# Sixteen weight subtractions on GpSimd instead of VectorE, and another buffer for the last weight tile

## The chip, the core and the metric

The kernel runs on one core of a Trainium2 chip. A core has five engines that run at the same time and meet by semaphores: TensorE (PE; its weight loads are listed as PEld), VectorE (DVE), ScalarE (ACT), GpSimd (POOL) and SyncE (SP), which here issues the DMAs. The metric is the device time of one execution in microseconds (us), as the median of several runs.

## The reference

Three parts follow each other, over 8 batches of 576 tokens, all in float32.

```python
# 1: attention in chunks of 64 tokens, 8 heads of 64
scores = scale * q_c @ k_c.T ; attn = softmax(scores) ; out = attn @ v_c
# 2: gated feed-forward, 512 -> 1024 -> 512, with a convolution of 3 taps along the tokens
h = maximum(x @ w_in, 0)
conv_out = sum_k conv_w[k] * shifted(h, k)
x = (h * sigmoid(conv_out)) @ w_out
# 3: FFT over tokens and features, normalisation, feed-forward 512 -> 2048 -> 512
u = x + real(fft(fft(x, axis=1), axis=2))
un = (u - mean(u)) / sqrt(var(u) + 1e-6)
y = u + maximum(un @ w_ch1, 0) @ w_ch2
```

The weights come as float64 bits, which the kernel turns into float32 itself.

## The kernel before

Matmuls run in a reduced float32 (`F32R`). To keep the precision, a factor is split into a high half and a low half: ScalarE casts the tile to `F32R` (the high half, `h`), VectorE subtracts that from the tile (the low half, `l`); this is `split` (L278). A product is then three matmuls: high times high, high times low, low times high.

The tokens of the first two parts go through in ten blocks (`NBLK`): one of 256 tokens, eight of 512, one of 256. Block 0 uses the plain float32 weights (`m_unit0`, L457, and the branch at L528); from block 1 on the split ones are used. In block 0 everything starts at once:

- `load_weight` (L344) fetches 16 tiles of 128x512, alternately of `w_in` and `w_out`, each as 512 KB of 64-bit words into a tile `wide`, and `to_float32` (L287) makes a float32 tile of it: L292, L293, L295 and L296 on VectorE, L294 on ScalarE. The float32 tiles lie in buffers that later hold other things (`early`, L340: `t`, `u`, `f..`, `fz`, `ds`, `xlo`, `xhi`, `dd`, `fw`), and so do some of the `wide` ones; the others share the ring of two buffers that is named `wide` in pool `w`.
- `attention` (L371) makes the scores (L393), their maxima (L398), the exponentials (L404), sums and division (L407 to L409), a transpose (L418, L421); `values` (L425) multiplies with v (L435) and, from block 1 on, splits the result: the cast at L442 on ScalarE, the subtraction at L444 on VectorE. There are two L444 for each half of a block's heads, so four for block 1.
- `m_step` (L451) multiplies with `w_in` (L459 in block 0, L468 later) for each of eight feature tiles f, goes through ReLU (L493), the middle tap (L498), the other two taps on VectorE (L488), tanh (L505) and the gate (L507), and from block 1 on splits the gated tile into `gh` and `gl` (L279, L280). GpSimd carries three edge columns from one block to the next (L492, L497). In block 0 it also calls `split_weight` (L353), which splits the weight tile that has just been used for the last time in float32.
- `x_step` (L518) multiplies with `w_out` (L531 in block 0, L537 later), and in block 0 splits that weight tile too.
- `load_dft` (L313) brings the transform matrices, with a cast on ScalarE (L323) and a subtraction on VectorE (L324); they land in the tile `fw`, which held the last weight tile in float32.

The order of the work is not that of the code. `Plan` records every operation with its engine, an estimated cost in nanoseconds, a priority and the tiles that it reads and writes. `emit` then plays the program through with these costs and gives each engine its instructions in the order that comes out. On the chip each engine runs its list strictly in order and waits at semaphores. A tile's next user waits for all users of the buffer before it.

Of the kernel before, what the change touches and what calls it, by code (L numbers as in the profile page):

```python
# [8 lines left out]
F32 = mybir.dt.float32  # L9
F32R = mybir.dt.float32r  # L10
I64 = mybir.dt.int64
U32 = mybir.dt.uint32
ACT = mybir.ActivationFunctionType
ALU = mybir.AluOpType
# [86 lines left out]
class Plan:  # L101
# [10 lines left out]
    def buf(self, pool, tag, bufs, shape, dtype=F32):  # L112
        return Buf(self, pool, tag, bufs, shape, dtype)

    def op(self, eng, cost, fn, prio, r=(), w=(), after=(), nbytes=0, spare=0):
        o = Op()
        o.spare = spare
        o.eng, o.cost, o.fn, o.prio, o.nbytes, o.seq = eng, cost, fn, prio, nbytes, len(self.ops)
        o.slots = [b for b in w if b.tag in self.ANY_ORDER and not b.writers]
        deps = {}  # L120
        for b in r:
            assert b.writers and not b.closed, b.tag
            for d in b.writers:
                deps[d] = True
        for b in w:
            assert not b.closed, b.tag
            if not b.writers:
                if b.pool in self.opened:
                    deps[self.opened[b.pool]] = True
                if b.before is not None:  # L130
                    for d in b.before.writers + b.before.readers:
                        deps[d] = True
                if b.previous is not None and b.previous not in w:
                    deps.setdefault(b.previous.writers[0], False)
            for d in b.writers + b.readers:
                deps[d] = True
        for d in after:
            deps[d] = True
        for b in r:
            for x in (b, b.base) if b.base else (b,):  # L140
                x.readers.append(o)
        for b in w:
            for x in (b, b.base) if b.base else (b,):
                x.writers.append(o)
        o.held = [b for b in {id(b): b for b in (*r, *w)}.values() if b.tag in self.ANY_ORDER]
        for b in o.held:
            b.left += 1
        o.deps, o.users = deps, []
        for d in deps:
            d.users.append(o)  # L150
        o.left, o.ready, o.end = len(deps), 0.0, None
        self.ops.append(o)
        return o
# [64 lines left out]
def act_cost(n, psum=False, scalars=0):  # L218
    return (51 if psum else 93) + n / 1.2 + 93 * scalars
# [7 lines left out]
def kernel(  # L227
# [15 lines left out]
    pe, dve, act, pool, sp = nc.tensor, nc.vector, nc.scalar, nc.gpsimd, nc.sync  # L243
    plan = Plan()
    buf, op = plan.buf, plan.op
# [23 lines left out]
    def load(dst, src, nbytes, prio, r=(), after=()):  # L269
        return op("SP", 450, lambda: sp.dma_start(out=dst(), in_=src()), prio, r=r, w=[dst], after=after, nbytes=nbytes)  # L270

    def vop(n, fn, prio, r, w, fast=False, scalars=0):
        return op("DVE", dve_cost(n, fast, scalars), fn, prio, r=r, w=w)

    def aop(n, fn, prio, r, w, psum=False, scalars=0, after=()):
        return op("ACT", act_cost(n, psum, scalars), fn, prio, r=r, w=w, after=after)

    def split(h, l, src, n, prio, psum=False, cut=lambda t: t, after=()):  # L278
        aop(n, lambda: act.copy(out=cut(h()), in_=cut(src())), prio, [src], [h], psum, after=after)  # L279
        vop(n, lambda: dve.tensor_tensor(cut(l()), cut(src()), cut(h()).bitcast(F32), op=ALU.subtract), prio, [src, h], [l])  # L280
# [6 lines left out]
    def to_float32(f, x, wide, n, prio, view=lambda t: t):  # L287

        word = lambda t, k: t.rearrange("p (n two) -> p n two", two=2)[:, :, k]
        lo, hi = lambda: word(wide().bitcast(U32), 0), lambda: word(wide().bitcast(U32), 1)  # L290
        ff, fb, xb = lambda: view(f()), lambda: view(f()).bitcast(U32), lambda: x().bitcast(U32)
        vop(n, lambda: dve.tensor_scalar(xb(), hi(), 3, 0x3FFFFFF8, op0=ALU.logical_shift_left, op1=ALU.bitwise_and), prio, [wide], [x], fast=True)  # L292
        vop(n, lambda: dve.scalar_tensor_tensor(fb(), in0=hi(), scalar=0xC0000000, in1=xb(), op0=ALU.bitwise_and, op1=ALU.bitwise_or), prio, [wide, x], [f])  # L293
        aop(n, lambda: act.activation(out=x(), in_=word(wide().bitcast(F32), 1), func=ACT.Abs), prio, [wide], [x])  # L294
        vop(n, lambda: dve.scalar_tensor_tensor(fb(), in0=lo(), scalar=29, in1=fb(), op0=ALU.logical_shift_right, op1=ALU.bitwise_or), prio, [wide, f], [f])  # L295
        vop(n, lambda: dve.scalar_tensor_tensor(ff(), in0=x(), scalar=LEAST_NORMAL, in1=ff(), op0=ALU.is_ge, op1=ALU.mult), prio, [x, f], [f])  # L296


    def weight(pool_name, tag, bufs):
        return tuple(buf(pool_name, tag + k, bufs, [128, 512], F32R) for k in "hl")  # L300
# [39 lines left out]
    early = [("s", "t", 2), ("s", "t", 2), ("s", "u", 2), ("s", "u", 2)]  # L340
# [3 lines left out]
    def load_weight(src, dst, prio):  # L344
        n = len(wi) + len(wo)
        f = buf(*early[n], [128, 512])
        dst.append([f])
        k = n % 5
        wide = buf(*(early[13 + k] if k < 3 and n < 13 else ("w", "wide", 2)), [128, 512], I64)
        load(wide, lambda: src, 524288, prio - (16.2 if n < 3 else 6))  # L350
        to_float32(f, buf("d", *(("wf", 2) if n % 3 else ("wx", 1)), [128, 512]), wide, 512, prio)

    def split_weight(w, tag, prio, after):  # L353
        f = w[0]
        w[:] = weight("w", tag, 8)
        split(*w, f, 512, prio, after=after)

# [91 lines left out]
    def m_step(i, f, prio):  # L451
# [19 lines left out]
        if i:  # L471
            done = op("PE", mm_cost(n, passes=12), m_unit, prio, r=[*wi[f], *(t.buf for hp in range(0, HP, 2) for t in x0[i, hp])], w=[acc], after=m_last)
            m_last[:] = [done]
        else:
            for hp in range(HP):
                done = op("PE", mm_cost(n, passes=4), lambda hp=hp: m_unit0(hp), prio, r=[wf, x0[i, hp][0].buf], w=[acc], after=() if hp else m_last)
                m_last[:] = m_last if hp else [done]
            split_weight(wi[f], "wi", prio + 6, [done])
# [34 lines left out]
    xacc, xlo, xhi, x_last, pieces = {}, {}, {}, {}, []  # L513
# [4 lines left out]
    def x_step(i, f, prio):  # L518
# [27 lines left out]
        if not i:  # L546
            split_weight(wo[f], "wo", prio + 6, [done])
# [484 lines left out]
    for f in range(FT):  # L1032
        load_weight(w_in[:, f, :], wi, -2 + f)
        load_weight(w_out[:, f, :], wo, 0 + f)
# [66 lines left out]
    for c in range(NCH):  # L1101
        t = start + span * c
        begun = []
        for g in range(FG):
            begun.append(group(c, g, t + 7 * g))
            if (c, g) in LATE:
                n = LATE.index((c, g))
# [125 lines left out]
```

## Time and profile before

| what | value |
|---|---|
| median of 3 runs | 1338.38 us (1335.93 to 1339.33) |
| profiled execution | 1338.54 us, span from first to last instruction 1336.8 us |
| mean granted TensorE clock | 0.995 of full speed |
| busy: PE, DVE, ACT, POOL | 1300.0, 1025.7, 765.7, 109.5 us |
| chain that ended last | PE 89%, DVE 6%, ACT 2% |

Busy time is the time in which an engine had an instruction under way. Consecutive instructions of one engine overlap a little in the records, so a sum of durations can be larger than the time that they took. The chain is followed back from the last instruction to what released each step. An engine's short idle times are listed with what ended them. Spans on GpSimd are rough, and a wait inside one of its instructions is part of its record.

### The profile page before, as it was taken

The page shows a single profiled execution, that of the slowest core. Times are in us where ns is not written, and L with a number is a line of the kernel's source. Part 1 is how long each engine was busy: PE and PEld are TensorE (multiplying, and loading weights), DVE is VectorE, ACT ScalarE, POOL GpSimd, SP SyncE. Part 2 cuts the span into 40 slices and gives each one's busy share as a digit, 9 for nine tenths or more (in the row PEclk, how much of TensorE's full clock was granted, in tenths as well). Part 3 has the DMA queues.
Part 4 walks back from the last instruction along what each step waited for, and adds up shares of the span by engine and source line. Part 5 has one row for each costly group of instructions (what it writes and reads, how often), then busy time and mean ns, then how long its engine had stood idle before and what let it go on. Part 6 is the DMA issues. An engine that isn't in the chain of part 4 may idle for free.

```text
span 1336.8 us, 26161 instructions
## 1 busy us (share of the span) xinstructions
PE 1300.0 (97%) x9888; PEld 1164.6 (87%) x9888; DVE 1025.7 (77%) x1832; ACT 765.7 (57%) x1902; POOL 109.5 (8%) x247
## 2 busy tenths in 40 slices
PE   5899999999999999999999999999999999999998
PEld 3678888788888888888999888888899999999998
DVE  7997979878886777787978768774598887777873
ACT  5968767657685755565766646566644333333331
POOL 1121312201120211120000000000000000000000
PEclk9999999999999999999999999999999999999999
DMA  9435142434423031337765766778655455455441
GB/s 327 148 128 174 42 149 92 159 104 146 148 72 99 17 111 45 100 128 233 220 211 184 227 193 198 209 223 279 195 177 168 137 174 161 139 174 147 154 142 40
DMA packets 155327, 206.29 MB, mean 154 GB/s; under 512 B 10304, under 2 KB 103104, under 8 KB 155200
## 3 DMA queue, kind: packets, MB, share of 16 engines
q1 hardware_dynamic: 155200, 204.61, 48.7%
q8 instruction: 78, 1.28, 0.4%
q14 instruction: 49, 0.40, 0.1%
HBM read 130.51 MB, written 74.06 MB: 153 GB/s over the span
## 4 chain that ended last, share of the span: by engine, by line
PE 89%; DVE 6%; ACT 2%; issue 1%; DMA 0%; SPq 0%; ACTq 0%; DVEq 0%
PE x L933 22%; PE x L1000 16%; PE o L468 14%; PE x L537 13%; PE o L1000 12%; PE o L933 4%; PE o L666 3%; PE o L699 2%; PE o L832 1%; PE o L721 1%; PE o L393 1%; DVE cv L488 1%; PE o L418 1%; PE o L435 1%; ACT th L279 0%
## 5 line engine op out<-in xcount | busy, mean ns | idle before, releaser
L279 ACT CAST sxh<-raw 128x1024 fp32r<-128x1024 f32 (+1 forms) x143 | 146.0, 1028 | 193.6 <-PE o L1000 84.3
L280 DVE TENSOR_TENSOR sxl<-raw,sxh 128x1024 fp32r<-128x1024 f32 (+1 forms) x143 | 169.3, 1193 | 26.7 <-ACT sxh L279 26.7
L933 PE MATMUL x<-sxh,th 128*128 128x512 f32 (+1 forms) x480 | 177.5, 370 | 0.8 <-ACT sum L917 0.6
L468 PE MATMUL o<-x,wih 128*128 128x512 f32 (+1 forms) x576 | 175.8, 388 | 1.8 <-ACT at L421 0.7
L933 PE MATMUL x<-sxh,tl 128*128 128x512 f32 (+1 forms) x480 | 176.6, 368 | 0.0
L933 PE MATMUL x<-sxl,th 128*128 128x512 f32 (+1 forms) x480 | 176.5, 368 | 0.0
L1000 PE MATMUL x<-tl,sxh 128*128 128x256 f32 x576 | 163.2, 283 | 0.0
L1000 PE MATMUL x<-th,sxl 128*128 128x256 f32 x576 | 163.1, 283 | 0.0
L1000 PE MATMUL x<-th,sxh 128*128 128x256 f32 x576 | 163.1, 283 | 0.0
L488 DVE SCALAR_TENSOR_TENSOR cv<-h,cw,cv 128x1 f32<-128x1 f32 (+30 forms) x272 | 129.0, 494 | 25.9 <-ACT cv L498 25.2
L468 PEld LDWEIGHTS o<-x,wih 128*128 128x128 f32 x576 | 104.1, 189 | 24.0 <-ACT h L493 1.5
L1000 PE MATMUL o<-tl,sxh 128*128 128x256 f32 x432 | 122.4, 283 | 0.0
L1000 PE MATMUL o<-th,sxl 128*128 128x256 f32 x432 | 122.4, 283 | 0.0
L1000 PE MATMUL o<-th,sxh 128*128 128x256 f32 x432 | 122.4, 283 | 0.0
L537 PE MATMUL x<-gh,woh 128*128 128x512 f32 (+1 forms) x288 | 112.6, 391 | 0.0
L1000 PEld LDWEIGHTS x<-th,sxh 128*128 128x128 f32 x576 | 110.7, 192 | 0.2
L1000 PEld LDWEIGHTS x<-tl,sxh 128*128 128x128 f32 x576 | 110.7, 192 | 0.0
L1000 PEld LDWEIGHTS x<-th,sxl 128*128 128x128 f32 x576 | 110.7, 192 | 0.0
L537 PE MATMUL x<-gh,wol 128*128 128x512 f32 (+1 forms) x288 | 110.3, 383 | 0.0
L468 PE MATMUL o<-x,wil 128*128 128x512 f32 (+1 forms) x288 | 110.0, 382 | 0.0
L537 PE MATMUL x<-gl,woh 128*128 128x512 f32 (+1 forms) x288 | 109.6, 381 | 0.2
L909 DVE TENSOR_TENSOR u<-x,u 128x256 f32<-128x256 f32 (+2 forms) x112 | 55.8, 498 | 67.4 <-PE x L1000 38.7
(280 smaller groups left out, 2955.4 us busy)
## 6 DMA issues: line engine op xcount, KB each, us to landing
raw<-h_scr SPq DMA_DIRECT2D x72, 512.0 KB, 5.0
h_scr<-sum SPq DMA_DIRECT2D x72, 256.0 KB, 3.0
u<-u_scr SPq DMA_DIRECT2D x66, 256.0 KB, 3.4
qk<-in_qk SPq DMA_DIRECT2D x32, 512.0 KB, 5.1
h_scr<-sum SPq DMA_DIRECT2D x48, 192.0 KB, 2.5
out_y<-u SPq DMA_DIRECT2D x35, 256.0 KB, 2.5
v<-in_v_in SPq DMA_DIRECT2D x32, 256.0 KB, 3.9
wide<-in_w_ch SPq DMA_DIRECT2D x16, 512.0 KB, 4.4
```

What stands on the lines that cost most here:

```text
L279: aop(n, lambda: act.copy(out=cut(h()), in_=cut(src())), prio, [src], [h], psum, after=after)
L280: vop(n, lambda: dve.tensor_tensor(cut(l()), cut(src()), cut(h()).bitcast(F32), op=ALU.subtract), prio, [src, h], [l])
L393: pe.matmul(s[h]()[half[u], 4 * w + 2 * p + j, :], t[half[h], w, 0, ks], t[half[h], w, 1, ks], start=True, stop=True)
L418: pe.transpose(tps()[:, k, :], flat[:, 512 * c + 128 * k:512 * c + 128 * k + 128], ident)
L468: pe.matmul(acc(), w[:, ws], x, start=k == 0, stop=k == 11)
L488: vop(hi - lo, lambda: dve.scalar_tensor_tensor(cv()[:, lo:hi], in0=h()[:, off + k - 1 + lo:off + k - 1 + hi], scalar=tap(k), in1=cv()[:, ...
L537: pe.matmul(accs[d](), w[:, dsl], x, start=f == 0 and k == 0, stop=f == FT - 1 and k == 2)
L666: pe.matmul(acc()[:rows, :], x, w, start=k == 0 and n == 0, stop=k == 1 and n == 2)
L699: pe.matmul(accs[sine]()[:rows, :], w, x, start=n == 0, stop=n == len(todo) - 1)
L909: vop(n, lambda: dve.tensor_tensor(cut(x()), acc(), cut(x()), op=ALU.add), prio, [acc, x], [x])
L933: pe.matmul(acc(), a, b, start=first and m == 0, stop=m == 5, skip_group_check=not first)
L1000: pe.matmul(acc(), a, b, start=first and m == 0 and gs[0] == 0, stop=gs[-1] == FG - 1 and m == len(todo) - 1, skip_group_check=not first)
```

## The change

`split_weight` no longer calls `split`. Its cast stays on ScalarE, and its subtraction, with the same operands, is recorded for GpSimd, with a cost of 1300 ns. `split` itself is not changed, so all other subtractions stay on VectorE. In `load_weight` the sixteenth 64-bit tile (n = 15) takes a buffer of the ring `xhi` in pool `s` in place of one of the two `wide` buffers.

```diff
@@ -346,14 +346,16 @@
         f = buf(*early[n], [128, 512])
         dst.append([f])
         k = n % 5
-        wide = buf(*(early[13 + k] if k < 3 and n < 13 else ("w", "wide", 2)), [128, 512], I64)
+        wide = buf(*(early[13 + k] if k < 3 and n < 13 else ("w", "wide", 2) if n < 15 else ("s", "xhi", 2)), [128, 512], I64)
         load(wide, lambda: src, 524288, prio - (16.2 if n < 3 else 6))
         to_float32(f, buf("d", *(("wf", 2) if n % 3 else ("wx", 1)), [128, 512]), wide, 512, prio)
 
     def split_weight(w, tag, prio, after):
         f = w[0]
         w[:] = weight("w", tag, 8)
-        split(*w, f, 512, prio, after=after)
+        h, l = w
+        aop(512, lambda: act.copy(out=h(), in_=f()), prio, [f], [h], after=after)
+        op("POOL", 1300, lambda: pool.tensor_tensor(out=l(), in0=f(), in1=h().bitcast(F32), op=ALU.subtract), prio, r=[f, h], w=[l])
 
 
 
```

Since costs and engines of sixteen operations are others, `emit` gives other orders for the first two blocks; behind them all engines have the order of before. Lines behind L357 are two higher in the changed kernel (L444 is L446 there, L505 is L507).

On VectorE, around the last two L444 of block 1 (output `x_957`), the order before has the subtractions of the low halves (`wil`, `wol`) between the other work:

```order
L295 SCALAR_TENSOR_TENSOR fw<-wide,fw 128x512
L444 TENSOR_TENSOR x_957<-o,x_950 128x4x128
L507 SCALAR_TENSOR_TENSOR gh<-cv,h 128x254
L296 SCALAR_TENSOR_TENSOR fw<-wx,fw 128x512
L280 TENSOR_TENSOR wil<-ds_634,wih 128x512
L280 TENSOR_TENSOR wol<-f_387,woh 128x512
L280 TENSOR_TENSOR wil<-xhi,wih 128x512
L444 TENSOR_TENSOR x_957<-o,x_950 128x4x128
L407 TENSOR_SCALAR sm<-sm 128x16
```

The same place in the changed kernel, where that output is `x_972`:

```order
L490 SCALAR_TENSOR_TENSOR cv<-h,cw,cv 128x254
L446 TENSOR_TENSOR x_972<-o,x_969 128x4x128
L509 SCALAR_TENSOR_TENSOR gh<-cv,h 128x254
L409 TENSOR_SCALAR sm<-sm 128x16
L400 TENSOR_REDUCE mx<-o 128x8
L446 TENSOR_TENSOR x_972<-o,x_969 128x4x128
```

The subtractions are gone, the conversion of the last tile (`fw`) stands further ahead, and a reduction for the next block's attention (L400) has moved in front of the last of these.

On GpSimd the beginning of the list before, behind the constants, is edge copies alone:

```order
masks.py:199 AFFINE_SELECT ident<-ident 128x128
L497 COPY hs<-h 128x3 x7
L492 COPY h<-hs 128x3
L497 COPY hs<-h 128x3
L492 COPY h<-hs 128x3
```

In the changed kernel the subtractions (L358) stand between them:

```order
masks.py:199 AFFINE_SELECT ident<-ident 128x128
L499 COPY hs<-h 128x3
L358 TENSOR_TENSOR wil<-t,wih 128x512
L499 COPY hs<-h 128x3 x2
L358 TENSOR_TENSOR wil<-u,wih 128x512
L358 TENSOR_TENSOR wil<-f_340,wih 128x512
L499 COPY hs<-h 128x3
L358 TENSOR_TENSOR wil<-f_437,wih 128x512
L358 TENSOR_TENSOR wol<-t,woh 128x512
L499 COPY hs<-h 128x3
L358 TENSOR_TENSOR wil<-fz,wih 128x512
L358 TENSOR_TENSOR wol<-u,woh 128x512
```

So the copies now have up to three subtractions ahead of them in the queue.

On ScalarE, at the beginning of block 1's feature tiles, the order before has the cast of the transform matrix (`dd<-fw`) behind the second `gh`:

```order
L505 ACTIVATE cv<-cv 128x512
L279 CAST gh<-cv 128x512
L505 ACTIVATE cv<-cv 128x512
L493 ACTIVATE h<-o 128x512
L294 ACTIVATE wx<-wide 128x512
L498 ACTIVATE cv<-h,cw 128x512
L279 CAST gh<-cv 128x512
L493 ACTIVATE h<-o 128x512
L323 CAST dd_1174<-fw 128x1032
```

In the changed kernel it stands ahead of the first:

```order
L507 ACTIVATE cv<-cv 128x512
L323 CAST dd_1115<-fw 128x1032
L279 CAST gh<-cv 128x512
L495 ACTIVATE h<-o 128x512
L500 ACTIVATE cv<-h,cw 128x512
```

On PE, block 1 had five feature tiles of L468 ahead of its first L537 and now has four.

## Rows read from the trace of the kernel before

**Rows 1.** The page, first part: busy us, share of the span, instructions.

```profile
PE 1300.0 (97%) x9888; PEld 1164.6 (87%) x9888; DVE 1025.7 (77%) x1832; ACT 765.7 (57%) x1902; POOL 109.5 (8%) x247
```

**Rows 2.** Windows: stretch, its length, busy us by engine, granted clock, DMA.

```profile
34.50:71.70 37.20, 30.48 (x430) 25.27 (x431) 37.20 (x79) 34.01 (x120) 7.74 (x9) 0.97 0.47 151
...
100.00:1336.00 1236.00, 1222.99 (x9108) 1103.23 (x9106) 936.21 (x1645) 695.42 (x1669) 91.49 (x221) 1.00 0.48 151
```

**Rows 3.** Chain of waits, 33 to 70 us: start, length, what.

```profile
33.27 0.34 DVE wx L292
33.61 0.39 DVE cv L488
34.60 0.60 DVE wil L280
...
35.29 0.33 DVE gh L507
...
36.32 1.13 DVE es L409
...
68.42 1.16 PE o L393 x62
```

**Rows 4.** Timeline of PE: start, length, instruction, idle time before and its releaser.

```profile
66.80 0.33 PE L393 MATMUL o<-qk 64*64 64x64 f32 x2 [1.18 <-ACT es L404]
...
69.51 3.50 PE L531 MATMUL x<-gh,fw 128*128 128x254 f32 x8
72.45 1.17 PE L468 MATMUL o<-x,wih 128*128 128x512 f32 x2
...
87.20 0.39 PE L537 MATMUL x<-gh,woh 128*128 128x512 f32 x1
```

**Rows 5.** Windows of L280 on VectorE alone, up to the fourth L444.

```profile
34.52:71.65 37.13, 6.70 (x10) 0.98 0.47 151
```

**Rows 6.** Timeline of GpSimd beside an idle VectorE.

```profile
208.06 0.76 POOL L596 CAST f<-f 128x66 fp32r<-128x66 f32 x4
208.76 0.18 POOL L497 COPY hs<-h 128x3 f32<-128x3 f32 x1
208.89 0.18 POOL L492 COPY h<-hs 128x3 f32<-128x3 f32 x1
```

**Rows 7.** Timelines of GpSimd and VectorE, around two long copies.

```profile
29.00 3.92 POOL L497 COPY hs<-h 128x3 f32<-128x3 f32 x1 [27.70 <-ACT h L493]
...
29.11 0.42 DVE L292 TENSOR_SCALAR wf<-fw 128x512 uint32<-128x512 uint32 x1
...
32.80 0.48 DVE L488 SCALAR_TENSOR_TENSOR cv<-h,cw,cv 128x253 f32<-128x253 f32 x1
...
68.83 2.33 POOL L492 COPY h<-hs 128x3 f32<-128x3 f32 x1 [5.28 <-DVE gh L507]
...
71.02 0.69 DVE L444 TENSOR_TENSOR x<-o,x 128x512 fp32r<-128x512 f32 x1
```

**Rows 8.** Timelines of GpSimd and VectorE, around four casts of GpSimd.

```profile
262.21 2.45 POOL L596 CAST f<-f 128x66 fp32r<-128x66 f32 x4
...
262.80 0.73 DVE L280 TENSOR_TENSOR gl<-cv,gh 128x512 fp32r<-128x512 f32 x1
```

**Rows 9.** Timelines of ScalarE and VectorE at the beginning of block 1.

```profile
82.60 0.62 ACT L279 CAST gh<-cv 128x512 fp32r<-128x512 f32 x1 [0.76 <-DVE cv L507]
...
86.32 1.05 ACT L323 CAST dd<-fw 128x1032 fp32r<-128x1032 f32 x1
...
83.88 0.69 DVE L280 TENSOR_TENSOR gl<-cv,gh 128x512 fp32r<-128x512 f32 x1
...
88.15 1.22 DVE L324 TENSOR_TENSOR dd<-fw,dd 128x1032 fp32r<-128x1032 f32 x1
```

**Rows 10.** DMA issues, 55 to 95 us: count, KB each, us from issue to landing.

```profile
fw<-in_dft_d SPq DMA_DIRECT2D x1, 516.0 KB, 3.4
```

**Rows 11.** Windows, as above, with the granted clock third from the end.

```profile
69.50:73.00 3.50, 3.50 (x15) 2.84 (x10) 3.50 (x8) 3.48 (x16) 1.65 (x1) 0.54 0.60 222
```

## The prediction

> **What bounds the kernel now.** The page comes first: PE is busy for 97% of the span [rows 1]. So nothing that another engine does counts unless PE stands still for it, and the next question is where PE does. The windows answer that: from 100 us to 1336 us PE is busy for 1222.99 of 1236.00 us, while in 34.5 to 71.7 us it is busy for 30.48 of 37.20 us, and there DVE is busy for all 37.20 us [rows 2]. The chain of waits then shows the order of events: up to 68 us it runs over DVE instructions without a break, from 68.42 us over PE [rows 3]. So the program has a DVE-bound beginning and a PE-bound rest. The turn is the first L468 matmul of block 1, at 72.45 us [rows 4], which needs both L444 pairs on DVE. A microsecond won or lost on DVE ahead of the fourth L444 (71.02 us) is, to first order, a microsecond of the kernel. The subtractions of L280 on weights lie there: ten of them between 34.52 us and the end of that L444 at 71.65 us, 6.70 us of recorded time [rows 5]. The records overlap by some 0.09 us; in the chain one takes 0.60 us [rows 3].
>
> **What is removed.** Sixteen DVE subtractions go. Ten stand ahead of the fourth L444: 10 x 0.60 = 6.0 us. The other six come behind it, when PE is dense; PE covered them, and their removal is worth nothing directly. The new order also brings one reduction (L398, 0.60 us) ahead of the fourth L444 and takes a few small ones away. In the new order the stretch from the place of the first subtraction to the fourth L444 holds 31 instructions of 0.60 us, 14 L488 of 0.39, 8 L507 of 0.33, 6 L292 of 0.34, 2 L409 of 1.13 us [rows 3] and some 0.7 us of tiny ones: 31.8 us, where it was 71.65 - 34.52 = 37.1 us. So DVE alone would be 5.3 us earlier.
>
> **What is added.** Sixteen subtractions of 128x512 on GpSimd, which has no such instruction in the trace. Its casts of 128x66 are the nearest row: beside an idle DVE four of them begin at 208.06 us and the copy of three elements behind them at 208.76 us, so each takes 0.175 us; that copy and the next begin 0.13 us apart [rows 6]. The difference over 63 elements is 0.7 ns an element. A subtraction reads two operands, 512 x 2 x 0.7 ns = 0.73 us, and 0.86 us with the fixed part. As a bound below, 0.62 us (the next paragraph says from what). As a bound above, 1.3 us, the number that the changed line itself gives its planner, which is no measurement.
>
> **Whether the two engines run side by side.** This decides the sign. A copy of 128x3 that began at 29.00 us took 3.92 us, and DVE ran without a gap from 29.11 us over L292, L293, L295 and L296 to the L488 at 32.80 us [rows 7]. The copy ended 0.12 us after that L488 began. Another, of 2.33 us from 68.83 us, ends 0.14 us after the L444 of 71.02 us began [rows 7]. In both, GpSimd got through only where DVE began an instruction that reads PSUM (L444) or one with a scalar operand per partition (L488), and not between instructions with two SBUF inputs. The opposite direction is there as well: at 262.80 us, with four GpSimd casts in flight, L280 takes 0.73 us, where one of the same shape took 0.69 us [rows 8, 9]. Some 0.04 us for 66 elements is 0.6 ns an element, the lower bound above (1024 x 0.6 = 0.62 us). So DVE waits for GpSimd too. The Trainium skill, "SBUF — State Buffer", section "Who interferes with whom", says that a VectorE instruction with two SBUF inputs and a GpSimd instruction that reads SBUF exclude each other, whichever comes second waiting for the whole of the first; the trace agrees, with 3.92 us of waiting for a copy of three elements.
>
> The sum follows. By the order of ScalarE's casts, 14 of the 16 subtractions become ready ahead of the fourth L444. In this stretch DVE offers 25 places to start: 14 L488, 5 L398, 4 L444, 2 L408. Nine of the 25 (L398, L444) read PSUM and run on beside GpSimd for their 0.60 us, so of 14 subtractions some five have 0.60 us free: 3.0 us. With a hold of 0.9 us (0.86 us, rounded up), DVE stands for 14 x 0.9 - 3.0 = 9.6 us. Less the 5.3 us: +4.3 us. With 0.62 us: 8.7 - 3.0 - 5.3 = +0.4 us. With 1.3 us: 18.2 - 3.0 - 5.3 = +9.9 us. With no hold at all: -5.3 us. I take 0.9 us, the row nearest in kind. The Trainium skill, "GPSIMD Engine Reference", section 3.1, gives 2.6 cycles an element for a two-input operation at 1.2 GHz; an estimate from it is 512 x 2.6 / 1.2 = 1.1 us, and the sum by it would be +7.1 us. No run here shows such an instruction yet.
>
> **The moved steps.** PE now runs four L468 groups of block 1 ahead of the first L537, not five; a group is 2.8 us. Before, L537 started at 87.20 us, and the first gl that it needs was done at 83.88 + 0.69 = 84.57 us: 2.6 us of slack [rows 4, 9]. One group fewer takes 2.8 us of it. ScalarE now has the cast of the transform matrix (L323, 1.05 us, before at 86.32 us) ahead of the first gh cast (82.60 us), and DVE its subtraction (1.22 us as recorded) ahead of the first gl [rows 9]. That makes gl some 0.9 us later, and PE waits for about 1 us. I add 1 us (0 to 2). L323 itself waits for a load into the tile that the last GpSimd subtraction frees; the load takes 3.4 us [rows 10]. If the last two subtractions end 3 us behind the first L468, it lands 3 to 4 us ahead of L323's turn on ScalarE (82.6 - 72.45 = 10 us behind that matmul). That is the cover; a GpSimd that is 4 us later uses it up.
>
> **The small ones.** The last tile's own buffer lets its load start earlier and its conversion run earlier; DVE has the same instructions, so on a DVE-bound path it is worth nothing. GpSimd's edge copies (L492, L497) now queue behind one or two subtractions each, and an h buffer comes free only after its L497. The order puts never more than three subtractions between two such copies, 3 x 0.9 = 2.7 us of work; ScalarE needs that buffer two steps of the block later. Nothing, or 1 us that the range holds. The granted clock was 0.54 from 69.5 to 73.0 us, that is mostly the lower level of 1.2 GHz [rows 11], after PE had waited 1.18 us and stood for DVE again at 68 us; eight L531 took 3.50 us there [rows 4], at full clock 3.5 x (1 - 0.54) = 1.6 us less. Another spacing of waits moves that by up to 1.6 us either way; I take zero.
>
> Profiled execution 1338.54 us (span 1336.8 us, 1.7 us around it), against a median of 1338.38 us: the two agree. 1338.5 + 4.3 + 1 = 1343.8, which I put at 1343.5 us.
>
> **Rivals.** (1) GpSimd runs beside DVE, the holds being an affair of tiny copies that wait for a slot. Then DVE gives its 5.3 us back, less up to 1 us for gl: 1333 to 1334 us, faster. For it: most DVE instructions beside a GpSimd copy keep their length. Against: those copies carry three elements, and a hold of three elements' length can't be seen. The sign turns at a hold of 0.5 us (9 x 0.5 = 4.5 us against 5.3 - 1). (2) GpSimd becomes the bound. Starting places are only 25, the subtractions wait for one each, and a hold of 1.3 us gives +9.9 us; then the last subtraction comes over 4 us late, L323 stands on ScalarE ahead of the first gh, and PE waits for 2 to 3 us more: 1349 to 1352 us. For it: the 3.92 us copy, and the in-order queue. Against: 16 x 1.3 = 21 us of work in 40 us. (3) The holds fall mostly beside PSUM readers and cancel against the saving: 1338 us, no change. It needs about 0.6 us a hold. That the change doesn't do what it says is excluded by the order: 16 subtractions stand on GpSimd, none on DVE.
>
> **The numbers.** 0.3% of 1338.4 us, about what a measurement tells from no change, is 4.0 us. The forecast (hold 0.6 to 1.1 us, 1339 to 1346 us) has 0.58, of which 0.36 lies above 1342.4 us. Rival 1 has 0.14 (0.12 faster), rival 2 0.17, rival 3 0.11. Slower: 0.36 + 0.17 = 0.53. Within: 0.22 + 0.11 + 0.02 = 0.35. Faster: 0.12. A range of 1335 to 1350 us leaves out most of rival 1 and the top of rival 2.
>
> **What would show it.** Right: GpSimd subtractions recorded at 1 us or more with a wait inside; DVE's L488, L293 or L295 in 34 to 75 us longer than 0.48 and 0.69 us by up to 1 us, where a subtraction begins; the first L468 at 75 to 80 us in place of 72.45 us; PE dense behind it, but for about 1 us at the first L537. Wrong: DVE instructions of their old lengths, the first L468 at 67 us. If that comes earlier and the time does not fall, the wait has moved behind it.

## The result and the profile after

| | before | after |
|---|---|---|
| median of 4 runs | 1337.45 us (1335.93 to 1339.33) | 1351.81 us (1350.62 to 1353.10) |
| profiled execution, span | 1338.54, 1336.8 us | 1353.10, 1351.1 us |

The changed kernel takes 1.0112 times as long (95% interval 1.0099 to 1.0125), 14.4 us more. The forecast had the sign, with 0.53 on slower, but 1343.5 us is 8 us short and the range of 1335 to 1350 us does not hold the time.

The first line of the page of the changed kernel answers to [rows 1]:

```profile
PE 1306.8 (97%) x9888; PEld 1169.7 (87%) x9888; DVE 1030.7 (76%) x1816; ACT 767.3 (57%) x1902; POOL 127.3 (9%) x263
```

VectorE executes sixteen instructions fewer and is busy for 5.0 us *more*. Sixteen subtractions of 0.60 us are 9.6 us that it no longer has, so its other instructions together are some 14.6 us longer.

The next two fences are the same windows of both kernels, the changed one first: the stretch, its length, busy us by engine, granted clock, DMA.

```profile
34.50:90.00 55.50, 41.48 (x449) 33.75 (x450) 48.70 (x75) 37.41 (x130) 28.16 (x25) 0.85 0.38 121
130.00:1350.00 1220.00, 1207.44 (x8911) 1090.72 (x8910) 923.26 (x1620) 681.51 (x1618) 87.52 (x216) 1.00 0.49 151
```

```profile
34.50:90.00 55.50, 48.78 (x505) 39.72 (x506) 54.42 (x111) 44.67 (x142) 9.53 (x15) 0.97 0.43 144
130.00:1335.00 1205.00, 1193.04 (x8797) 1079.11 (x8795) 913.75 (x1600) 671.64 (x1577) 87.55 (x214) 1.00 0.48 150
```

From 130 us on PE stands for 12.6 us against 12.0. The loss is made ahead of that: in the same 55.5 us PE gets through 449 recorded instructions in place of 505. The granted clock there is 0.85 in place of 0.97, that is more time at the lower level of 1.2 GHz in a stretch with more waits. PE's idle time over the whole span grows by 7.5 us (44.3 against 36.8 us, span less busy time); its busy time grows by 6.8 us for the same 9888 matmuls. Most of both lies ahead of the first matmul of block 1's feature tiles (L468 at 72.45 us before, L470 at 85.97 us after), as the windows up to it show, the changed kernel first:

```profile
0.00:85.97 85.97, 55.40 (x664) 43.45 (x665) 72.17 (x128) 54.66 (x205) 29.21 (x32) 0.90 0.58 198
```

```profile
0.00:72.45 72.45, 49.42 (x664) 39.38 (x665) 63.01 (x136) 53.42 (x205) 12.37 (x16) 0.96 0.68 234
```

The same 664 recorded matmuls are busy for 6.0 us more, at a granted clock of 0.90 in place of 0.96, and PE stands for 7.5 us more.

GpSimd in the changed kernel, by the timeline (start, length, instruction, idle before and its releaser):

```profile
39.18 1.36 POOL L358 TENSOR_TENSOR wil<-u,wih 128x512 fp32r<-128x512 f32 x1 [1.11 <-ACT wih L357]
...
74.49 1.29 POOL L358 TENSOR_TENSOR wil<-dd,wih 128x512 fp32r<-128x512 f32 x1
75.74 1.44 POOL L358 TENSOR_TENSOR wol<-xlo,woh 128x512 fp32r<-128x512 f32 x1
```

And VectorE beside it:

```profile
30.11 1.49 DVE L292 TENSOR_SCALAR wf<-wide 128x512 uint32<-128x512 uint32 x1
...
40.75 1.75 DVE L296 SCALAR_TENSOR_TENSOR f<-wf,f 128x512 f32<-128x512 f32 x1
...
46.71 0.88 DVE L490 SCALAR_TENSOR_TENSOR cv<-h,cw,cv 128x253 f32<-128x253 f32 x1
...
60.69 0.68 DVE L296 SCALAR_TENSOR_TENSOR xhi<-wx,xhi 128x512 f32<-128x512 f32 x1
61.29 1.75 DVE L296 SCALAR_TENSOR_TENSOR xlo<-wf,xlo 128x512 f32<-128x512 f32 x1
...
71.19 1.76 DVE L295 SCALAR_TENSOR_TENSOR fw<-xhi,fw 128x512 uint32<-128x512 uint32 x1
...
75.98 1.23 DVE L401 TENSOR_SCALAR mx<-mx 128x16 f32<-128x16 f32 x1
```

Each subtraction makes one VectorE instruction longer, nearly always by the same amount: L292 from 0.42 to 1.49 us, L296 from 0.68 to 1.75, L295 from 0.68 to 1.76, and even the maximum over 128x16 (L401) from 0.17 to 1.23. That is a hold of 1.07 us. Three holds are cut short, to 0.41 (46.71 us), 0.71 and 0.58 us, where a reduction from PSUM (L400) ran beside the beginning of the subtraction. Over the fourteen subtractions up to 77.2 us the excess of these instructions over their usual lengths sums to 13.3 us.

What the path did is in the chain of waits of the changed kernel (start, length, what), which answers to [rows 3]:

```profile
76.06 1.16 DVE mx L401
77.22 0.02 issue
77.24 2.48 ACT es L406 x16
79.72 0.48 ACT x L444
80.21 0.02 issue
80.23 0.70 DVE x L446
80.94 0.04 issue
80.98 1.98 PE o L395 x62
82.96 3.37 PE x L533 x8
86.32 11.19 PE o L470 x48
97.52 2.56 PE x L539 x11
```

The first L470 (L468 before) starts at 85.97 us by the timeline, 13.5 us later than in [rows 4]. The path now runs over the maxima of block 2's scores (L401), then ScalarE: eight exponentials of block 2 with the eight reads of their sums (L406, x16 in the chain), and only then the cast that block 1's third L446 waits for (L444, which is L442 before). VectorE stands still for 2.64 us ahead of that L446.

The kernel before has the same queue. Its timelines of VectorE, ScalarE and PE:

```profile
64.07 0.17 DVE L399 TENSOR_SCALAR mx<-mx 128x16 f32<-128x16 f32 x1
...
67.68 0.69 DVE L444 TENSOR_TENSOR x<-o,x 128x512 fp32r<-128x512 f32 x1
...
63.70 0.51 ACT L498 ACTIVATE cv<-h,cw 128x254 f32<-128x254 f32 x1
64.27 0.31 ACT L404 ACTIVATE es<-o,mx 128x64 f32<-128x64 f32 x1
...
66.60 0.62 ACT L442 CAST x<-o 128x512 fp32r<-128x512 f32 x1
...
70.24 0.69 ACT L442 CAST x<-o 128x512 fp32r<-128x512 f32 x1
...
68.42 1.16 PE L393 MATMUL o<-qk 64*64 64x64 f32 x62 [1.30 <-DVE x L444]
```

ScalarE ends a convolution tap (L498) at 64.21 us and VectorE the maxima at 64.24 us, so the two are level there. ScalarE starts its exponentials at 64.27 us, works without a gap, and ends the third cast for block 1 at 67.22 us; the third L444, which uses it, begins at 67.68 us. So VectorE's work between the maxima and the third L444 lay beside the exponentials, with 0.46 us to spare.

It is this third L444 that PE waits for: it releases the L393 of 68.42 us, behind which eight L531 and the first L468 follow in PE's list without a gap [rows 4]. The fourth L444 (71.02 us [rows 7], its cast done at 70.93 us) ends at 71.71 us, 0.74 us ahead of the first L468, and isn't in the chain.

### The profile page after: what moved, and what is told of

It reads as the page before. It is cut to its first block, busy times and chain, and to the rows that moved or that the text cites. A ratio compares the mean times of both kernels' runs of the same rounds, so it can differ in the third digit from the quotient of the medians.

```text
span 1351.1 us, 26168 instructions
## 1 busy us (share of the span) xinstructions
PE 1306.8 (97%) x9888; PEld 1169.7 (87%) x9888; DVE 1030.7 (76%) x1816; ACT 767.3 (57%) x1902; POOL 127.3 (9%) x263
## 4 chain that ended last, share of the span: by engine, by line
PE 89%; DVE 6%; ACT 3%; issue 1%; DMA 0%; SPq 0%; ACTq 0%; DVEq 0%
PE x L935 21%; PE x L1002 15%; PE o L470 14%; PE x L539 13%; PE o L1002 12%; PE o L935 4%; PE o L668 3%; PE o L701 2%; DVE cv L490 1%; PE o L723 1%; PE o L834 1%; PE o L395 1%; PE o L420 1%; PE o L437 1%; ACT es L406 1%
## 5 line engine op out<-in xcount | busy, mean ns | idle before, releaser
L280 DVE TENSOR_TENSOR sxl<-raw,sxh 128x1024 fp32r<-128x1024 f32 (+1 forms) x143 | 169.4, 1194 | 26.1 <-ACT sxh L279 25.9
L470 PE MATMUL o<-x,wih 128*128 128x512 f32 (+1 forms) x576 | 175.3, 387 | 1.8 <-ACT at L423 0.7
L490 DVE SCALAR_TENSOR_TENSOR cv<-h,cw,cv 128x1 f32<-128x1 f32 (+30 forms) x272 | 133.9, 512 | 29.0 <-ACT cv L500 28.5
L470 PEld LDWEIGHTS o<-x,wih 128*128 128x128 f32 x576 | 104.0, 188 | 23.7 <-ACT h L495 1.1
L539 PE MATMUL x<-gh,woh 128*128 128x512 f32 (+1 forms) x288 | 112.5, 391 | 0.0
L539 PE MATMUL x<-gh,wol 128*128 128x512 f32 (+1 forms) x288 | 110.2, 383 | 0.0
L470 PE MATMUL o<-x,wil 128*128 128x512 f32 (+1 forms) x288 | 110.0, 382 | 0.0
L539 PE MATMUL x<-gl,woh 128*128 128x512 f32 (+1 forms) x288 | 109.5, 380 | 0.2
```

Source lines behind the costliest of these rows:

```text
L470: pe.matmul(acc(), w[:, ws], x, start=k == 0, stop=k == 11)
L490: vop(hi - lo, lambda: dve.scalar_tensor_tensor(cv()[:, lo:hi], in0=h()[:, off + k - 1 + lo:off + k - 1 + hi], scalar=tap(k), in1=cv()[:, ...
L539: pe.matmul(accs[d](), w[:, dsl], x, start=f == 0 and k == 0, stop=f == FT - 1 and k == 2)
```

## The experiments

Two theories. **A**: a GpSimd subtraction of this size holds VectorE for 1.07 us; what counts is VectorE's work up to the maxima of block 2's first scores (L399 at 64.07 us, L401 in the changed kernel; "the second pair's maxima" in the expectations), since ScalarE's queue carries the path from there. **P**, the step of the prediction: every microsecond of VectorE ahead of the fourth L444 counts, so the subtractions' removal was worth its 5.3 us and the loss is that much more than 14 us elsewhere. **B**, in some expectations, puts 4 to 5 us of the loss on the new order itself. Other letters in the expectations are variants of these, as told there. The kernels follow in the order in which they narrow the cause.

**The changed order without the work on GpSimd.** Everything as in the changed kernel, but a subtraction covers two columns, and the matmuls take the high half in the low half's place (not shown in the cut of the edit).

```diff
-  pool.tensor_tensor(out=l(), in0=f(), in1=h().bitcast(F32), op=ALU.subtract)
+  pool.tensor_tensor(out=l()[:, :2], in0=f()[:, :2], in1=h()[:, :2].bitcast(F32), op=ALU.subtract)
```

> The changed kernel's order and buffers, but each GpSimd subtraction works on 2 columns, and the matmuls take the high half in the low half's place (the low halves of the weights are left out). Theory A (each GpSimd subtraction holds VectorE for 1.07 us, 13.3 us in sum, and nothing else is lost; the path ends at the second pair's maxima L399/L401, to which the two orders have 29.7 and 29.2 us of VectorE steps): 1337 to 1339 us, no change against before. Theory B (the new order itself costs some 4 to 5 us, since VectorE stands 2.6 and 1.7 us for ScalarE ahead of the last two subtractions of x; the holds only explain 9 us): 1342 to 1344 us. Theory P (as the prediction had it: VectorE bounds up to the fourth L444): 1333 to 1334 us.

Measured: 1337.24 us, ratio to before 0.9999 (0.9990 to 1.0009). The timelines:

```profile
63.63 0.17 DVE L401 TENSOR_SCALAR mx<-mx 128x16 f32<-128x16 f32 x1
66.82 0.69 DVE L446 TENSOR_TENSOR x<-o,x 128x512 fp32r<-128x512 f32 x1 [2.58 <-ACT x L444]
...
68.65 1.98 PE L533 MATMUL x<-gh,fw 128*128 128x254 f32 x8
70.28 11.54 PE L470 MATMUL o<-x,wih 128*128 128x512 f32 x48
```

This settles most of it. With the sixteen subtractions gone from VectorE and hardly anything put on GpSimd, the kernel is no faster than before. The maxima come 0.44 us earlier than before and the fourth L446 (70.19 us) 0.83 us, not 5.3; VectorE stands for 2.58 us in front of the third L446 and waits for ScalarE. P (1333 to 1334 us) and B (1342 to 1344 us) fall. The lines of the old length are back, and VectorE's busy time on the page is 1016.7 us, 14.0 us less than in the changed kernel, which has the same instructions there. So all of the loss, and no more, comes from the size of the GpSimd instruction. (This profiled execution is 2.4 us faster than the one of before, most of it eight L533 at full clock, 1.98 us at a granted clock of 1.00 against 3.50 us in [rows 4]; the medians don't differ.)

**The order of before, with VectorE's subtractions cut.**

```diff
-        split(*w, f, 512, prio, after=after)
+        h, l = w
+        aop(512, lambda: act.copy(out=h(), in_=f()), prio, [f], [h], after=after)
+        vop(512, lambda: dve.tensor_tensor(l()[:, :2], f()[:, :2], h()[:, :2].bitcast(F32), op=ALU.subtract), prio, [f, h], [l])
```

The matmuls take the high half in the low half's place here too.

> The kernel before in its own order, with each of the 16 VectorE subtractions cut to 2 columns and the high half used in place of the low half (low halves of the weights left out). It gives the most that taking them off VectorE can be worth. Theory A: 5 of them stand ahead of the second pair's maxima, 5 x 0.54 = 2.7 us less: about 1335.5 us. Theory P: ten of them stand ahead of the fourth L444, 5.4 us less: about 1333 us. Theory B says nothing of this one.

Measured: 1336.66 us, 0.9992 (0.9983 to 1.0001). The timelines:

```profile
62.57 0.17 DVE L401 TENSOR_SCALAR mx<-mx 128x16 f32<-128x16 f32 x1
...
64.16 0.30 ACT L406 ACTIVATE es<-o,mx 128x64 f32<-128x64 f32 x1
...
70.83 0.69 DVE L446 TENSOR_TENSOR x<-o,x 128x512 fp32r<-128x512 f32 x1 [1.86 <-ACT x L444]
...
72.21 14.09 PE L470 MATMUL o<-x,wih 128*128 128x512 f32 x58
```

The subtractions on VectorE are worth at most about 2 us of time by the interval, and about 1 by the medians. P had 5.4 us and falls. A had 2.7 us and is too high as well: the maxima are 1.5 us earlier, but the exponentials start only 0.11 us earlier than before (64.27 us), since ScalarE has a ReLU, a cast and a convolution tap ahead of them by the chain of waits; the first L470 is 0.24 us earlier. So time taken away ahead of the maxima gains next to nothing.

**The changed order, with the subtractions executed by VectorE.** The planner still counts them for GpSimd.

```diff
-  op("POOL", 1300, lambda: pool.tensor_tensor(out=l(), in0=f(), ...
+  op("POOL", 1300, lambda: dve.tensor_tensor(l(), f(), ...
```

> The changed kernel's plan (costs, priorities, buffers), but the subtraction is issued on VectorE at the point of the program where the plan has it for GpSimd. No holds, 12 subtractions of 0.60 us ahead of the second pair's maxima. Theory A: 36.4 us of VectorE steps up to there in place of 29.7: +6.7 us, about 1345 us, that is 6 to 7 us faster than on GpSimd. Theory B: +4 to 5 us for the order and +5 for the subtractions, 1347 to 1349 us. Theory P: 39.7 in place of 37.1 us, +2.6 us, 1341 us.

Measured: 1345.66 us, 1.0064 (1.0048 to 1.0079), as A said. The timelines:

```profile
71.39 0.17 DVE L401 TENSOR_SCALAR mx<-mx 128x16 f32<-128x16 f32 x1
...
80.42 1.31 PE L470 MATMUL o<-x,wih 128*128 128x512 f32 x2
```

The maxima are 7.3 us later than before, the first L470 8.0 us, the median 8.0 us. Two things follow. What is added ahead of the maxima costs the kernel its whole length, though what is taken away there gained next to nothing in the run before. And the same subtractions in the same plan cost 6 us less on VectorE (1345.66 us) than on GpSimd (1351.81 us): a 1.07 us hold against 0.60 us of own work.

**The second edit alone.** `split_weight` as before, only the last weight tile's own buffer.

> The second edit alone: the last 64-bit tile in its own buffer, all subtractions on VectorE. Theory A: 31.0 us of VectorE steps up to the second pair's maxima in place of 29.7, since the last tile's conversion moves ahead of them: +1.3 us, about 1339.7 us, within the noise. Theory P: 38.5 in place of 37.1 us up to the fourth L444, the same +1.4 us. If the buffer matters by itself (the load later in the way of others), it is off from this by more than 3 us.

Measured: 1339.77 us, 1.0020 (1.0009 to 1.0031). A and P say the same here. The timelines show why the free-looking buffer costs 2 us: the maxima (L399) are at 65.03 us, 0.96 us later, because the last tile's conversion is now planned ahead of them, the third L444 is 0.83 us later, and the first L468 is at 74.36 us, 1.91 us later. The rest is PE's own: its 62 score matmuls (L393) behind that L444 take 1.98 us in place of 1.16, at a granted clock of 0.50 in place of 1.00, and the eight L531 0.24 us more.

**How the hold goes with the operands.** GpSimd copies one operand in place of subtracting two:

```diff
-  pool.tensor_tensor(out=l(), in0=f(), in1=h().bitcast(F32), op=ALU.subtract)
+  pool.tensor_copy(out=l(), in_=f())
```

> The changed kernel, each GpSimd subtraction replaced by a GpSimd copy of the same 128x512 (one SBUF input; the low halves of the weights are a copy of the tile, not the difference). How the hold grows with what GpSimd reads. Theory A1 (the hold goes with the elements read: 1.07 us for two operands, so 0.53 us for one): 14 x 0.53 = 7.4 us less some overlap, 1343 to 1345 us. Theory A2 (a fixed hold for an instruction, whatever it reads): 13 us, 1350 to 1352 us. Theory A3 (only two operands hold, as one fits between VectorE's reads): 1337 to 1339 us.

Measured: 1341.18 us, 1.0033 (1.0021 to 1.0045). The timelines of GpSimd and VectorE:

```profile
66.45 0.60 POOL L358 CAST wil<-dd 128x512 fp32r<-128x512 f32 x1
...
61.75 0.83 DVE L292 TENSOR_SCALAR wx<-xhi 128x512 uint32<-128x512 uint32 x1
...
67.37 0.60 DVE L401 TENSOR_SCALAR mx<-mx 128x16 f32<-128x16 f32 x1
```

L292 takes 0.41 us more, L401 0.43. One operand holds VectorE for 0.42 us, 0.82 ns an element; two hold it for 1.07 us, 2.09 ns an element, 2.5 times as long. Half of the two-operand hold, 0.53 us, was too much for the copy, so the time lies a little below A1's 1343 to 1345 us, and far from A2's 1350 to 1352.

**GpSimd writes only.** A memset of the same tile, which reads nothing:

```diff
-  pool.tensor_tensor(out=l(), in0=f(), in1=h().bitcast(F32), op=ALU.subtract)
+  pool.memset(l().bitcast(F32), 0.0)
```

> The changed kernel, each GpSimd subtraction replaced by a GpSimd memset of 128x512 to zero (no input; the low halves of the weights are zero). Theory A1 (only what GpSimd reads holds VectorE's instructions with two SBUF inputs): no hold there, at most some for the L292 that run at two elements a cycle: 1337 to 1339 us, no change. Rival (a GpSimd write holds as well): some 14 x 0.3 to 0.5 us = 4 to 7 us, 1341 to 1345 us.

Measured: 1337.80 us, 1.0005 (0.9996 to 1.0014). A memset is recorded for 0.52 us, about as long as the copy, and costs nothing that can be measured. VectorE's instructions with two SBUF inputs keep their lengths. Only TENSOR_SCALAR instructions grew, for example in the timelines:

```profile
28.34 0.81 DVE L292 TENSOR_SCALAR wf<-fw 128x512 uint32<-128x512 uint32 x1
...
54.47 0.94 DVE L292 TENSOR_SCALAR wf<-wide 128x512 uint32<-128x512 uint32 x1
```

These are 0.39 and 0.52 us above L292's 0.42; all such excess sums to 1.5 us. So it is GpSimd's reading that holds VectorE's two-input instructions. The Trainium skill, "SBUF — State Buffer", section "Who interferes with whom", draws the same line: two SBUF inputs on VectorE collide with a GpSimd instruction that reads, not with one that only writes, and `tensor_scalar` can enter a mode that takes the whole shared pair. The traces of these kernels agree.

**Is it ScalarE's queue that ends the path?** This edit is called the gate below. The order of before, and the scores of block 2's first head pair wait for block 1's last L444, so that the exponentials can't be planned ahead of block 1's casts:

```diff
-  op("PE", 310 + 470 * nw, qk_unit, prio, r=qks, w=s)
+  op("PE", 310 + 470 * nw, qk_unit, prio, r=qks, w=s, after=x1_done if (i, q) == (2, 0) else ())
```

> The kernel before with one more dependency in the plan: the scores of block 2's first pair of heads wait for block 1's last subtraction of x (L444), so their exponentials no longer stand ahead of block 1's last casts of x (L442) on ScalarE. All subtractions on VectorE, each with its cost of before. Theory A (behind the maxima at 64 us the turn to block 1 hangs on ScalarE's exponentials, not on VectorE): x is there 3 to 5 us earlier, PE fills with L468, 1333 to 1336 us. Rival (VectorE's total work bounds the turn, as theory P had it): PE starts L468 earlier and then waits for the low halves and for gh and gl, 1337 to 1339 us, no change.

Measured: 1333.77 us, 0.9972 (0.9963 to 0.9982), faster than both kernels. Timelines, and the window of 34.5 to 90 us:

```profile
56.67 0.69 DVE L444 TENSOR_TENSOR x<-o,x 128x512 fp32r<-128x512 f32 x1
58.26 0.69 DVE L444 TENSOR_TENSOR x<-o,x 128x512 fp32r<-128x512 f32 x1
...
60.05 0.82 PE L470 MATMUL o<-x,wih 128*128 128x512 f32 x2
```

```profile
34.50:90.00 55.50, 52.04 (x527) 42.45 (x528) 55.50 (x115) 46.32 (x146) 12.08 (x19) 1.00 0.42 141
```

The fourth L444 starts 12.8 us earlier, though all sixteen subtractions are VectorE's, PE has its L470 at 60 us and stays at full clock. VectorE is busy for the whole 55.5 us, so it is still the busiest beside PE, yet PE is busy for 3.3 us more than before. The order of the work, not the amount on VectorE, set the start of the dense part.

A's time is met and the rival's 1337 to 1339 us is not, but A's reason is only a part: it gave 3 to 5 us for x, not 12.8. The added dependency changed VectorE's order as well: by the timeline two of the subtractions stand ahead of the fourth L444, where there were ten, and the last tile's conversion and block 2's maxima come behind it. How much of the 3.6 us is ScalarE's queue and how much VectorE's shorter list ahead of that L444, the run doesn't tell.

**The gate, with VectorE's subtractions planned later.** Priorities of the subtractions 1 (`w_in`) and 9 (`w_out`) later.

> As the gate alone, and the weight subtractions on VectorE have later priorities (w_in's by 1, w_out's by 9 places), since w_out's low halves are first used 14 us after the first L468. Theory A: with the gate, VectorE's load ahead of x counts again only in so far as block 0's gated tiles are late, so about 1 to 2 us better than the gate alone, 1332 to 1335 us. Rival (the low halves then come too late for the first L537): no better, or up to 2 us worse, than the gate alone.

Measured: 1333.53 us, 0.9971 (0.9959 to 0.9982): the same as the gate alone; the 1 to 2 us of A don't show. Once the gate is there, where VectorE has the subtractions is worth nothing that can be measured.

**The first edit alone**, GpSimd's subtractions and the ring of two `wide` buffers for all.

> The first edit alone: subtractions on GpSimd, the last 64-bit tile in the ring of two buffers as before. Theory A: 26.4 us of VectorE steps up to the second pair's maxima (29.2 with both edits, 29.7 before), as the last tile's conversion then stands behind them, and the same holds of 1.07 us: 12 to 13.3 us, so +9 to +10 us against before, 1346.5 to 1348.5 us. Theory Q (the queue on GpSimd and not VectorE's steps decides): the same as with both edits, 1351 to 1352 us.

Measured: 1349.83 us, 1.0092 (1.0064 to 1.0120). It is about 2 us below the whole change, the size of the second edit alone, and a little more than expected. The interval reaches the whole change's, so these two are not told apart well. The first edit makes most of the loss. Its path isn't quite A's: the maxima end at 70.72 us, 6.5 us later than before, but the first L470 starts at 83.03 us, 10.6 us later; between them the chain of waits goes over block 2's exponentials, the division of its softmax (L411), the third L446 and a gate (L509) on VectorE.

**The gate and GpSimd's subtractions.**

> The gate with the subtractions on GpSimd, the last tile in the ring of two as before. Theory A: the turn to block 1 comes earlier, with some 6 to 8 holds ahead of it; but VectorE works without a gap up to 90 us there too, and PE, which now starts block 1 before block 0 is done, follows VectorE's gated tiles of both. 16 x (1.07 - 0.60) = 7.5 us is the most that the holds can cost against the gate alone: 1337 to 1341 us, 3 to 7 us slower than the gate alone. Rival (with the gate the holds are covered by PE's block 1): 1333 to 1335 us. Theory Q (GpSimd's queue, up to three subtractions ahead of an edge copy, holds up h): over 1343 us.

Measured: 1351.00 us, 1.0102 (1.0080 to 1.0124). A's 1337 to 1341 us fails: the subtractions on GpSimd cost 17 us against the gate alone. Its timeline of VectorE and its windows:

```profile
48.85 1.23 DVE L401 TENSOR_SCALAR mx<-mx 128x16 f32<-128x16 f32 x1
...
67.53 0.68 DVE L446 TENSOR_TENSOR x<-o,x 128x512 fp32r<-128x512 f32 x1
```

```profile
34.50:90.00 55.50, 43.91 (x416) 34.66 (x416) 49.04 (x77) 37.82 (x125) 23.72 (x26) 0.94 0.35 116
90.00:130.00 40.00, 38.17 (x347) 30.53 (x348) 37.04 (x72) 29.48 (x82) 13.30 (x14) 1.00 0.46 138
```

The holds are there (fifteen subtractions up to 85 us, 13.9 us in sum), and block 1's L446 come 10.9 us later than with the gate alone. PE then still stands for 1.8 us between 90 and 130 us, where the gate alone left it no idle time. In the gated order VectorE has no free time up to 90 us, so a likely reading is that every hold delays all that stands behind it, in an order whose planner knew of none; the expectation had counted them only up to the one point where the path leaves VectorE. Of the 14.3 us between the two profiled executions 10.5 lie ahead of block 1's first matmul with `w_in` (70.57 against 60.05 us), the other 3.8 behind it. The time lies where theory Q had it, but ahead of 90 us the timelines show no more than 0.4 us in which ScalarE waits for an edge copy; behind 90 us the chain does go over one such copy (2.94 us at 120.76 us), so Q isn't excluded there. How the 17 us divide between holds, the new order and the waits behind 90 us was not tried and stays open.

## Why the prediction was right and wrong

**Right: the mechanism and the sign.** The prediction read from [rows 7] that the two engines exclude each other, and asked for L488, L293 or L295 longer by up to 1 us where a subtraction begins. That is what the rows show, with L292, L296 and L401 among them. It placed the loss ahead of the first L468 and a dense PE behind it, and the windows agree; but the first L470 at 85.97 us lies beyond the 75 to 80 us that it asked for.

**Wrong: the step "a microsecond won or lost on DVE ahead of the fourth L444 is, to first order, a microsecond of the kernel".** It holds for what is added up to block 2's maxima, where VectorE is the last to come; it doesn't hold for what is taken away. The term for the removal, −5.3 us, was −0.4 us at the maxima (63.63 against 64.07 us with two-column subtractions) and nothing in the median. This is the largest error of the sum, 4.9 us. Two readings led to it. The chain of [rows 3] goes over to PE at 68.42 us, released by the third L444; the fourth isn't in it, and three of the ten subtractions begin behind that point (69.21 to 70.42 us). And the chain was taken as the whole path. A chain names the releaser that came last; here ScalarE came 0.03 us ahead of VectorE at the maxima and 0.46 us ahead of it at the third L444. These rows of ScalarE were in the trace and weren't looked for. The new order also spent part of what was won: the last tile's conversion now lies ahead of the maxima.

**Too small: the hold.** The prediction took 0.9 us, with bounds of 0.62 and 1.3 us; it is 1.07 us, which makes 2.4 us for fourteen. The row it stood on, casts of 66 elements beside an idle VectorE, gives 0.7 ns an element for one operand, where the hold of a copy of 512 gives 0.82; and two operands cost 2.5 times one, not twice. The sentence by the Trainium skill, "GPSIMD Engine Reference", section 3.1, 2.6 cycles an element and an estimate of 1.1 us, had the better figure; the hold of 1.07 us agrees with it.

**Too large: the cover.** Five PSUM readers were to hide 0.60 us each, 3.0 us in all. Three did, and 15.0 − 13.3 = 1.7 us were hidden in all. Nor did GpSimd get in only at the places that the prediction counted: the L296 of 61.29 us, with two SBUF inputs, was held right behind another one.

**Too large: 1 us for `gl`.** By the timelines the first `gl` is done at 96.70 us, and the first L539 starts at 97.35 us: the slack fell from 2.6 us to 0.65 us, but was not used up, and by the chain PE goes from L470 into L539 without a wait. The term was 0. The clock term of 0 is borne out for the eight L533 (3.44 us, against 3.50 us for L531 in [rows 4]), but not for the 62 score matmuls ahead of them: L395 took 1.98 us in the chain, where L393 took 1.16 us [rows 3], at a granted clock of 0.50 in place of 1.00.

The sum by measured terms: −0.4 + 13.3 = 12.9 us, and 13.0 us measured at the end of the maxima (77.21 against 64.24 us); 0.5 us more up to the first L470 (13.5 us); and 0.8 us behind it, which makes the 14.3 us by which the span grew.

**The rivals.** Rival 2 (1349 to 1352 us) gave the right time by the wrong way: there was no 1.3 us hold, and no stall of PE behind L323. Its condition, a GpSimd that is the bound, was not met: GpSimd was idle for 8.74 us at one place ahead of 59.16 us while it waited for ScalarE, and up to 100 us no engine waits for the result of a GpSimd instruction by the releasers of the timelines. Rivals 1 and 3 needed a hold of 0.5 to 0.6 us, and fall with the 1.07 us.

## What to carry to other kernels

Before work is moved off an engine, look in the trace at every queue that feeds the end of the path, not only at the one that the chain names: what is removed is worth no more than the distance to the second releaser (here 0.03 us at the maxima and 0.46 us at the third L444). Price an elementwise instruction moved from VectorE to GpSimd by the time that it holds VectorE; where that (here 1.07 us) is longer than VectorE's own execution (0.60 us), the move costs time wherever VectorE is on the path. The gain lay in the order: one added dependency, which kept the next block's softmax behind this block's last casts, was worth 3.6 us with no work moved to another engine.

## What the runs showed of the hardware that was not expected

- The hold does not depend on the VectorE instruction that meets it: one of 0.17 us waits for 1.06 us like one of 0.68 us.
- Two SBUF operands on GpSimd hold VectorE for 2.09 ns an element of 512, one for 0.82 ns. A GpSimd instruction is recorded for longer than it holds VectorE: mostly 1.27 to 1.45 us against 1.07, and 0.60 against 0.42.
- A memset on GpSimd (0.52 us recorded) leaves VectorE's two-input instructions alone, but lengthened some TENSOR_SCALAR by 0.39 to 0.52 us.
